# Second network of a fused attention kernel: when the second batch is transposed, in which order the first pair's products run, and which engine makes sums and low parts

## The chip, the cores and the metric

The kernel runs on one core of a Trainium2 chip. The metric is the device time of one execution in microseconds (us). The core has a matrix engine (TensorE, PE in the profile; PEld is its loading of weights), three engines for elementwise work (VectorE or DVE, ScalarE or ACT, GpSimd or POOL) and a queue for transfers (SyncE or SP). Each engine works off its own instructions in order and waits by semaphores for the others. Matrix products go into PSUM, from which VectorE and ScalarE read; everything else lies in SBUF.

## The reference

Attention over 512 local and 32 global rows in each of 4 batches, then two feed-forward networks. The change touches the second one alone:

```python
def _moe2_ref(x, w_in, conv_w, w_out):      # x: (4, 544, 512), d_ff = 1024
    h = np.maximum(x @ w_in, 0.0)
    hp = np.concatenate([zeros, h, zeros], axis=1)
    conv_out = sum(conv_w[k][None, None, :] * hp[:, k:k + S, :] for k in range(3))
    gate = 1.0 / (1.0 + np.exp(-conv_out))
    return (h * gate @ w_out).astype(np.float32)
```

All is float32. A product is made from high and low parts in a reduced float32 format (float32r): w_hi x_hi + w_hi x_lo + w_lo x_hi, three matmuls for one.

## The kernel before

Attention and the first network fill the span up to some 543 us. Each finished block of 128 rows of the first network is scaled and added by VectorE (L741) and stored to the scratch tensor `yscr` in memory (`store_y`, L690, SP's queue); the 32 global rows of each batch are stored there too. The last two blocks belong to batch 3.

The second network goes through the batches 0 to 3, and in each through four pairs `p` of hidden blocks of 128 channels (`NPR` = 4, so 16 pairs, called pair 0 to pair 15 here). For a batch, its 544 rows must lie transposed, as channels by rows. `y_load` (L875) brings a block of rows from `yscr` into `yr` (three buffers), `y_part` (L880) transposes it with four TensorE instructions (L886) into PSUM, from which ScalarE copies it to `yT` (L888). A batch has five blocks, 32 rows and four of 128. Batch 0 is transposed and prepared within the first network. For batch b + 1, pair 0 of batch b loads the blocks 0 to 2 and pair 1 the blocks 3 and 4 (`YP`, L1085); in each pair `turn()` takes one block after T1, one after B22 and one after the output block that follows.

The product x @ w_in of a pair is made in a form with seven instead of eight partial products, each of two 272-column halves: sums of the rows' quarters (`y_sums`, L903: T3, T2, T1 and T4, each 128x544) and of the weights' quarters are made first. For batches 1 to 3 GpSimd makes these sums at the head of pair 2. Then in pair 3, as soon as a product of the old batch is done, ScalarE makes the high part of the new batch's factor and VectorE or (T3, T4, B22) GpSimd the low part (`y_split`, L915), in the place of the old.

`hidden` (L1015) is one pair: the products B11, T2, T3, T1, T4, B21, B22, each six matmuls at L999, with additions between them on VectorE (L1029, L1034, L1039, L1044, L1054) and ScalarE (L1024, L1049). T4 goes on in the PSUM bank of T3 after L1034 has read it (u3), B21 in that of B11, B22 in that of T1. The additions are put 60 instructions ahead in priority (`ahead(B_ADD)`). The tile scheduler orders each engine's instructions by readiness and priority; only TensorE's order in the second network is held to the program's (`keep_order`). `issue_after` (through `behind`) puts an instruction behind another in the issue order of one engine without waiting for its end: the products come behind `mark["first"]`, the last matmul of the last hidden block of the first network.

`gate` (L1001) then makes, for each of the pair's two hidden blocks, the three-tap convolution (L1003 ScalarE, L1004 and L1005 VectorE), the sigmoid (L1006 ScalarE, whose function table is loaded before the first), the product with h (L1007 VectorE), the high part `gh` (ScalarE) and the low part `gl` (GpSimd, both by `split`, L115). `output` (L1073) multiplies a hidden block with its rows of w_out: twelve matmuls (L1061 and L1062 take `gh`, L1063 `gl`). In pair i the output of hidden block 2i - 3 stands between T1 and T4, and that of 2i - 2 after B22. At the end stand the output of the last blocks, that of the global rows of all batches together (`orem`), the copies out of PSUM and the stores.

## Time and profile before

| | us |
|---|---|
| median of 3 runs | 749.65 (749.33 to 752.72) |
| profiled execution | 747.93 |
| its span, first to last instruction | 746.1 |
| TensorE busy in the span | 725.2 (97%) |
| VectorE, ScalarE, GpSimd busy | 490.7, 411.1, 261.1 |
| granted TensorE clock, mean | 0.995 |

The profile is of one execution. The chain of waits goes back from the last instruction to what released each one; the timeline lists instructions by start; windows give each engine's busy time and the granted clock in a stretch of the span. Matmuls overlap, so the distance from one to the next counts and not the length of one. "issue" is time in which the engine named waited for nothing that the profile shows as an instruction of another engine.

### The profile page before, as it was taken

The page shows a single profiled execution, that of the slowest core. Times are in us where ns is not written, and L with a number is a line of the kernel's source. Part 1 is how long each engine was busy: PE and PEld are TensorE (multiplying, and loading weights), DVE is VectorE, ACT ScalarE, POOL GpSimd, SP SyncE. Part 2 cuts the span into 40 slices and gives each one's busy share as a digit, 9 for nine tenths or more (in the row PEclk, how much of TensorE's full clock was granted, in tenths as well). Part 3 has the DMA queues.
Part 4 walks back from the last instruction along what each step waited for, and adds up shares of the span by engine and source line. Part 5 has one row for each costly group of instructions (what it writes and reads, how often), then busy time and mean ns, then how long its engine had stood idle before and what let it go on. Part 6 is the DMA issues. An engine that isn't in the chain of part 4 may idle for free.

```text
span 746.1 us, 13077 instructions
## 1 busy us (share of the span) xinstructions
PE 725.2 (97%) x4745; PEld 650.7 (87%) x4745; DVE 490.7 (66%) x1077; ACT 411.1 (55%) x951; POOL 261.1 (35%) x301
## 2 busy tenths in 40 slices
PE   9999999999999999999999999999959999999997
PEld 5778899999899999999999999988948888888985
DVE  4889974655767666665567526726738969869651
ACT  6768743545565655555445423425545675666742
POOL 1013032434444443444334300002327646565331
PEclk9999999999999999999999999999989999999999
DMA  9992241323333433343232103135121030110101
GB/s 370 424 412 83 57 159 33 118 86 100 111 101 104 120 109 95 84 135 90 80 92 85 36 1 127 58 109 192 58 91 29 1 117 1 29 56 1 58 1 70
DMA packets 31120, 76.18 MB, mean 102 GB/s; under 512 B 3776, under 2 KB 10704, under 8 KB 28496
## 3 DMA queue, kind: packets, MB, share of 16 engines
q1 hardware_dynamic: 30528, 74.52, 30.2%
q8 instruction: 37, 0.61, 0.3%
q10 hardware_dynamic: 528, 0.84, 0.3%
q14 instruction: 27, 0.22, 0.1%
HBM read 66.43 MB, written 8.91 MB: 101 GB/s over the span
## 4 chain that ended last, share of the span: by engine, by line
PE 56%; DVE 6%; issue 5%; ACT 3%; POOL 2%; DMA 1%; ACTq 0%; DVEq 0%; POOLq 0%; SPq 0%
PE ph L709 17%; PE yps L733 6%; PE yps L738 6%; PE yps L734 5%; DVE c L1005 2%; PE pv L999 2%; PE po L337 2%; PE po L1063 2%; PE po L1061 2%; PE po L1062 2%; PE pt L316 2%; POOL gl L115 1%; PE pz L999 1%; PE px L999 1%; DVE c L1004 1%
## 5 line engine op out<-in xcount | busy, mean ns | idle before, releaser
L709 PE MATMUL ph<-xe,w 128*128 128x256 f32 (+1 forms) x768 | 119.8, 298 | 0.9 <-ACT w L159 0.9
L115 POOL TENSOR_TENSOR kl<-raw,kh 128x448 fp32r<-128x448 f32 (+2 forms) x59 | 70.6, 1196 | 133.8 <-ACT kh L108 110.7
L709 PEld LDWEIGHTS ph<-xe,w 128*128 128x128 f32 x768 | 108.4, 188 | 6.2 <-ACT w L159 1.2
L733 PE MATMUL yps<-w,hh 128*128 128x512 f32 x272 | 110.5, 406 | 0.9 <-ACT hh L718 0.4
L709 PE MATMUL ph<-xo,w 128*128 128x256 f32 x768 | 108.2, 284 | 0.0
L734 PE MATMUL yps<-w,hh 128*128 128x512 f32 x272 | 107.7, 396 | 0.0
L709 PEld LDWEIGHTS ph<-xo,w 128*128 128x128 f32 x768 | 101.0, 188 | 4.1
L718 ACT ACTIVATE hh<-ph 128x256 fp32r<-128x256 f32 (+1 forms) x128 | 50.1, 393 | 65.4 <-PE ph L709 59.7
L719 DVE SCALAR_TENSOR_TENSOR hl<-ph,hh 128x256 fp32r<-128x256 f32 x112 | 46.6, 417 | 54.1 <-ACT hh L718 53.1
L115 POOL TENSOR_TENSOR gl<-c,gh 128x544 fp32r<-128x544 f32 x32 | 45.4, 1419 | 78.9 <-ACT gh L108 78.9
L738 PE MATMUL yps<-w,hl 128*128 128x512 f32 x224 | 72.5, 398 | 0.0
L303 ACT ACTIVATE sm<-sm,nm 128x192 f32<-128x192 f32 (+1 forms) x128 | 58.6, 460 | 12.3 <-DVE nm L294 12.0
L294 DVE CUSTOM_DVE_ANT_0 sm<-ps,mask 128x192 f32<-128x192 f32 (+1 forms) x128 | 42.5, 368 | 33.6 <-PE ps L291 22.8
L108 ACT ACTIVATE kh<-raw 128x448 fp32r<-128x448 f32 (+2 forms) x59 | 34.3, 581 | 45.7 <-issue 26.8
L733 PEld LDWEIGHTS yps<-w,hh 128*128 128x128 f32 x272 | 51.2, 188 | 8.8 <-ACT hh L718 1.8
L734 PEld LDWEIGHTS yps<-w,hh 128*128 128x128 f32 x272 | 51.3, 188 | 5.6
L1061 PE MATMUL po<-w,gh 128*128 128x512 f32 x128 | 51.1, 399 | 0.0
L1063 PE MATMUL po<-w,gl 128*128 128x512 f32 x128 | 50.6, 395 | 0.5 <-POOL gl L115 0.5
L1062 PE MATMUL po<-w,gh 128*128 128x512 f32 x128 | 50.7, 396 | 0.0
L261 POOL TENSOR_TENSOR qs<-raw,qs 64x256 fp32r<-64x256 f32 x43 | 33.6, 782 | 46.4 <-DVE qs L260 17.6
L738 PEld LDWEIGHTS yps<-w,hl 128*128 128x128 f32 x224 | 41.1, 188 | 8.7
L321 ACT ACTIVATE ptsb<-pt 128x384 f32<-128x384 f32 (+1 forms) x64 | 34.3, 538 | 25.1 <-PE pt L316 24.6
(186 smaller groups left out, 1572.0 us busy)
## 6 DMA issues: line engine op xcount, KB each, us to landing
wraw<-w SPq DMA_DIRECT2D x16, 1024.0 KB, 16.9
raw<-a_m SPq DMA_DIRECT2D x23, 352.0 KB, 3.0
raw<-a_e SPq DMA_DIRECT2D x20, 320.0 KB, 2.9
raw<-g_qk SPq DMA_DIRECT2D x16, 304.0 KB, 2.8
rawg<-g_v SPq DMA_DIRECT2D x16, 280.0 KB, 2.9
wraw<-w_in SPq DMA_DIRECT2D x8, 512.0 KB, 3.6
yr<-yscr SPq DMA_DIRECT2D x16, 256.0 KB, 2.7
wraw<-w_out SPq DMA_DIRECT2D x4, 1024.0 KB, 7.3
```

What stands on the lines that cost most here:

```text
L115: e_lo.tensor_tensor(lo, src, f32(hi), op=ALU.subtract)
L294: DVE.tensor_tensor_reduce(out=s, in0=ps[j][:, :w], in1=mask[:, self.m0:self.m0 + w], scale=-0.125, scalar=BIG, op0=ALU.add, op1=ALU.min, ...
L303: ACT.activation(s, s, AF.Exp, bias=self.nm[:, j:j + 1], scale=-1.0, accum_out=xt.sums[:, h:h + 1])
L709: e = PE.matmul(ph[:, :n], w[:, d * P:(d + 1) * P], x[:, d], start=m == 0, stop=m == 3 * NDC - 1)
L718: ACT.activation(hh, ph[:, :n], AF.Relu)
L719: DVE.scalar_tensor_tensor(hl, ph[:, :n], 0.0, f32(hh), op0=ALU.max, op1=ALU.subtract)
L733: PE.matmul(yps[i], hh[:, tk], wh[:, DM:], start=edge(k, -1), stop=False)
L734: PE.matmul(yps[i], hh[:, tk], wl[:, DM:], start=False, stop=False)
L738: PE.matmul(yps[i], hl[:, tk], wh[:, DM:], start=False, stop=edge(k, 1))
L1061: PE.matmul(o, gh, wh, start=first, stop=False)
L1062: PE.matmul(o, gh, wl, start=False, stop=False)
L1063: PE.matmul(o, gl, wh, start=False, stop=last)
```

## The change

`B_ADD` is 300 and not 60. `mark["last"]` is the last matmul of the first network's second layer; the products from T3 on come behind it in TensorE's order, B11 and T2 behind `mark["first"]` as before. For batch 1 the loads and transposes begin in pair 1 with two blocks (0 and 1) and end in pair 2 with three; for batches 2 and 3 they stay in the first two pairs of the batch before. The sums are made by VectorE: for batch 1 all four at B11 of pair 3, for the others one at each product from B11 on in the third pair of the batch before. In pair 0 the product B21 comes ahead of T4. In pair 15 VectorE makes the low parts `gl` of both gates.

```diff
--- before.py
+++ after.py
@@ -53,7 +53,7 @@
 HOLD = 2
 HB2 = 2
 PREP = 220
-B_ADD = 60
+B_ADD = 300
 
 XB = 4
 PTB = 2
@@ -735,7 +735,7 @@
 
             for i, key in enumerate(chunks[ci]):
                 tk = slice(i * P, (i + 1) * P)
-                PE.matmul(yps[i], hl[:, tk], wh[:, DM:], start=False, stop=edge(k, 1))
+                mark["last"] = PE.matmul(yps[i], hl[:, tk], wh[:, DM:], start=False, stop=edge(k, 1)).ins
                 if edge(k, 1):
                     x = xtiles[key].x
                     DVE.scalar_tensor_tensor(x, yps[i], xtiles[key].rstd, x, op0=ALU.mult, op1=ALU.add)
@@ -900,17 +900,17 @@
             parts.append(slots2[i // 3][:, i % 3])
         yc[n] = parts
 
-    def y_sums(yT, t, e):
+    def y_sums(yT, t):
 
         ya, yb = [y[:, d] for y, _ in yT for d in (slice(0, 2), slice(2, 4))] if len(yT) == 1 else [y for y, _ in yT]
         u0, u1 = slice(0, HB), slice(HB, S)
         b11, b12, b21, b22 = ya[:, :, u0], ya[:, :, u1], yb[:, :, u0], yb[:, :, u1]
         t3, t2, t4 = t
         ysrc.update({"B11": b11, "T2": t2, "T3": t3, "T1": b12, "T4": t4, "B21": b21, "B22": b22})
-        return [lambda: e.tensor_tensor(t3, b22, b12, op=ALU.subtract),
-                lambda: e.tensor_tensor(t2, t3, b11, op=ALU.add),
-                lambda: e.tensor_tensor(b12, b12, b11, op=ALU.subtract),
-                lambda: e.tensor_tensor(t4, b21, t2, op=ALU.subtract)]
+        return [lambda: DVE.tensor_tensor(t3, b22, b12, op=ALU.subtract),
+                lambda: DVE.tensor_tensor(t2, t3, b11, op=ALU.add),
+                lambda: DVE.tensor_tensor(b12, b12, b11, op=ALU.subtract),
+                lambda: DVE.tensor_tensor(t4, b21, t2, op=ALU.subtract)]
 
     def y_split(n):
         split(*yc[n], ysrc[n], ACT, POOL if Y_NAMES.index(n) in (2, 4, 6) else DVE)
@@ -926,7 +926,7 @@
     def y0_sums(k):
         if k == 0:
             t = wpool.tile([P, 3, 2, HB], F32, tag="w4", name="yt")
-            ysrc["ops"] = y_sums(yT0, [t[:, i] for i in range(3)], DVE)
+            ysrc["ops"] = y_sums(yT0, [t[:, i] for i in range(3)])
         ysrc["ops"][k]()
 
     def y0_split(n):
@@ -988,17 +988,17 @@
     gts, ops = {}, {}
     U0, U1 = slice(1, 1 + HB), slice(1 + HB, 1 + S)
 
-    def product(ps, w, k, n, start):
+    def product(ps, w, k, n, start, key="last"):
 
         yh, yl = yc[n]
         for d in range(2):
             c = slice(k * EIGHTH + d * P, k * EIGHTH + (d + 1) * P)
             wh, wl = w[:, 0, c], w[:, 1, c]
             for m, (wx_, y) in enumerate(((wh, yh), (wh, yl), (wl, yh))):
-                with behind("first"):
+                with behind(key):
                     PE.matmul(ps, wx_, y[:, d], start=start and d + m == 0, stop=d + m == 3, skip_group_check=True)
 
-    def gate(b, f, h):
+    def gate(b, f, h, e=POOL):
         c = gpool.tile([P, S], F32, tag="c", name="c")
         ACT.activation(c, h[:, 0:S], AF.Copy, scale=cw[:, 3 * f:3 * f + 1])
         DVE.scalar_tensor_tensor(c, h[:, 1:S + 1], cw[:, 3 * f + 1:3 * f + 2], c, op0=ALU.mult, op1=ALU.add)
@@ -1007,7 +1007,7 @@
         DVE.tensor_tensor(c, h[:, 1:S + 1], c, op=ALU.mult)
         gh = gpool.tile([P, S], F32R, tag="gh", name="gh", bufs=4)
         gl = gpool.tile([P, S], F32R, tag="gl", name="gl", bufs=4)
-        split(gh, gl, c, ACT, POOL)
+        split(gh, gl, c, ACT, e)
         POOL.tensor_copy(grem_h[:, f, b * SG:(b + 1) * SG], f32(gh[:, :SG]))
         POOL.tensor_copy(grem_l[:, f, b * SG:(b + 1) * SG], f32(gl[:, :SG]))
         gts[b, f] = gh, gl
@@ -1018,13 +1018,14 @@
         n = b * NPR + p
         he, ho = hs[2 * n % 4], hs[(2 * n + 1) % 4]
         p1s, u2, u3 = (us[:, n % 2 * 3 + i] for i in range(3))
+        e = DVE if n == B * NPR - 1 else POOL
         px = ps_x.tile([P, HB], F32, tag="px", name="px")
-        product(px, a, 0, "B11", True)
+        product(px, a, 0, "B11", True, "first")
         with ahead(B_ADD):
             ACT.activation(p1s, px, AF.Copy)
         at("B11")
         py = ps_x.tile([P, HB], F32, tag="py", name="py")
-        product(py, x, 1, "T2", True)
+        product(py, x, 1, "T2", True, "first")
         with ahead(B_ADD):
             DVE.tensor_tensor(u2, py, p1s, op=ALU.add)
         at("T2")
@@ -1039,22 +1040,29 @@
             DVE.tensor_tensor(he[:, U1], pz, u3, op=ALU.add)
         at("T1")
         at(0)
-        product(pv, a, 3, "T4", False)
-        with ahead(B_ADD):
-            DVE.tensor_tensor(he[:, U0], pv, u2, op=ALU.add)
-        ACT.activation(he[:, 1:1 + S], he[:, 1:1 + S], AF.Relu)
-        at("T4")
-        product(px, a, 1, "B21", False)
-        with ahead(B_ADD):
-            ACT.activation(ho[:, U0], px, AF.Relu)
-        at("B21")
-        gate(b, 2 * p, he)
+
+        def t4():
+            product(pv, a, 3, "T4", False)
+            with ahead(B_ADD):
+                DVE.tensor_tensor(he[:, U0], pv, u2, op=ALU.add)
+            ACT.activation(he[:, 1:1 + S], he[:, 1:1 + S], AF.Relu)
+            at("T4")
+
+        def b21():
+            product(px, a, 1, "B21", False)
+            with ahead(B_ADD):
+                ACT.activation(ho[:, U0], px, AF.Relu)
+            at("B21")
+
+        for part in (t4, b21) if n else (b21, t4):
+            part()
+        gate(b, 2 * p, he, e)
         product(pz, x, 2, "B22", False)
         with ahead(B_ADD):
             DVE.tensor_tensor(ho[:, U1], pz, u2, op=ALU.add)
         ACT.activation(ho[:, U1], ho[:, U1], AF.Relu)
         at("B22")
-        gate(b, 2 * p + 1, ho)
+        gate(b, 2 * p + 1, ho, e)
 
     def mm_o(o, gh, gl, f, first, last):
         wh, wl = (w[:, f % 2 * DM:(f % 2 + 1) * DM] for w in wt["o", f // 2])
@@ -1082,20 +1090,24 @@
                 (ACT if e is DVE else SP).dma_start(out[b, SG + t * P:SG + (t + 1) * P, :], emit(ops[b][t], e))
 
     steps = [(b, f) for b in range(B) for f in range(NF2)]
-    YP = [(0, 1, 2), (3, 4)]
     second = len(traced())
+    yT, sums, parts = None, [], []
     for i in range(B * NPR):
         b, p = divmod(i, NPR)
         more = b + 1 < B
-        if more and p == 0:
-            yT = [(gpool.tile([P, NDC, S], F32, tag="yT", name="yT", bufs=1), slice(0, NDC))]
-        parts = list(YP[p]) if more and p < 2 else []
-        for k in parts:
-            y_load(b + 1, k, gpool, "yr", 3)
-        if more and p == 2:
-            t = [gpool.tile([P, 2, HB], F32, tag=f"yt{k}", name="yt", bufs=1) for k in range(3)]
-            for op in y_sums(yT, t, POOL):
-                op()
+        if more:
+            k = p - (b == 0)
+            if k == 0:
+                yT = [(gpool.tile([P, NDC, S], F32, tag="yT", name="yT", bufs=1), slice(0, NDC))]
+                todo = list(range(NT + 1))
+            if 0 <= k < 2:
+                n = 2 if b == 0 and k == 0 else 3
+                parts, todo = todo[:n], todo[n:]
+                for x in parts:
+                    y_load(b + 1, x, gpool, "yr", 3)
+            if k == 2:
+                t = [gpool.tile([P, 2, HB], F32, tag=f"yt{k}", name="yt", bufs=1) for k in range(3)]
+                sums = y_sums(yT, t)
 
         def turn():
             if parts:
@@ -1106,7 +1118,13 @@
                 if 2 * i >= 3:
                     output(*steps[2 * i - 3])
                 turn()
-            elif more and p == 3:
+                return
+            if sums:
+                sums.pop(0)()
+                if more and p == 3 and n == "B11":
+                    while sums:
+                        sums.pop(0)()
+            if more and p == 3:
                 y_split(n)
 
         hidden(b, p, at)
@@ -1114,6 +1132,7 @@
         if 2 * i >= 2:
             output(*steps[2 * i - 2])
         turn()
+        assert not parts
     output(*steps[-3])
     o = ps_v.tile([P, DM], F32, tag="pv", name="orem")
     output(*steps[-2])
```

## Rows read from the trace of the kernel before

**Rows 1.** The page, part 1: busy time, share, instructions.

```profile
PE 725.2 (97%) x4745; PEld 650.7 (87%) x4745; DVE 490.7 (66%) x1077; ACT 411.1 (55%) x951; POOL 261.1 (35%) x301
```

**Rows 2.** Chain of waits, 545 us: start, length, engine, tile, line.

```profile
543.79 1.40 DVE x L741 x2
545.22 2.02 DMA yscr<-x
547.24 2.40 issue
```

**Rows 3.** Windows, mostly by pair: stretch, length, engines' busy time, clock, DMA.

```profile
543.66:549.64 5.98, 0.00 (x2) 0.03 (x1) 2.32 (x5) 0.84 (x1) 2.60 (x2) 0.82 0.40 125
549.64:567.50 17.86, 15.03 (x92) 13.98 (x93) 9.68 (x15) 11.94 (x21) 5.64 (x8) 0.87 0.27 83
567.50:579.20 11.70, 11.12 (x68) 9.67 (x67) 10.35 (x13) 5.98 (x11) 9.27 (x9) 1.00 0.00 1
579.20:590.04 10.84, 10.84 (x67) 9.75 (x66) 9.69 (x13) 8.32 (x16) 7.24 (x8) 1.00 0.01 2
...
661.06:672.80 11.74, 11.16 (x68) 9.71 (x67) 10.39 (x13) 6.02 (x11) 9.27 (x9) 1.00 0.00 1
...
716.20:727.04 10.84, 10.84 (x67) 9.75 (x66) 6.43 (x12) 5.49 (x11) 3.45 (x6) 1.00 0.00 0
```

**Rows 4.** Chain of waits: one product, one transposed block of 128 rows.

```profile
579.36 0.75 PE px L999 x6
...
598.82 0.44 PE pty L886 x4
```

**Rows 5.** Windows of 2 us, the clock: pause's end, and 559.

```profile
548.00:550.00 2.00, 0.36 (x4) 0.39 (x4) 0.00 (x0) 0.00 (x0) 0.00 (x0) 0.50 0.67 176
...
558.00:560.00 2.00, 0.77 (x6) 0.78 (x7) 1.28 (x2) 1.97 (x5) 0.00 (x0) 1.00 0.00 0
```

**Rows 6.** Timeline, first gate: start, length, engine, line, operation, [idle before].

```profile
551.94 0.44 DVE L1044 TENSOR_TENSOR hs<-pv,us 128x272 f32<-128x272 f32 x1 [5.86 <-PE pv L999]
...
555.00 0.77 DVE L1005 SCALAR_TENSOR_TENSOR c<-hs,cw,c 128x544 f32<-128x544 f32 x1
...
556.74 1.28 ACT L1006 ACT_TABLE_LOAD   x1
...
558.03 0.66 ACT L1006 ACTIVATE c<-c 128x544 f32<-128x544 f32 x1
...
559.23 1.01 PE L999 MATMUL py<-yc,wx 128*128 128x272 f32 x6 [2.15 <-ACT yT L888]
...
560.22 1.37 POOL L115 TENSOR_TENSOR gl<-c,gh 128x544 fp32r<-128x544 f32 x1 [13.01 <-ACT gh L108]
```

**Rows 7.** Timeline, pair 15: a low part, the output taking it.

```profile
729.57 1.35 POOL L115 TENSOR_TENSOR gl<-c,gh 128x544 fp32r<-128x544 f32 x1 [7.40 <-ACT gh L108]
...
730.98 0.50 PE L1063 MATMUL po<-w,gl 128*128 128x512 f32 x1 [0.51 <-POOL gl L115]
```

**Rows 8.** Timeline, VectorE at the pause: the add making u3.

```profile
545.11 0.43 DVE L1034 TENSOR_TENSOR us<-pv,us 128x272 f32<-128x272 f32 x1
```

**Rows 9.** Groups by line, 540 to 746: count, busy us, mean ns.

```profile
L1029 DVE TENSOR_TENSOR us<-py,us 128x272 f32<-128x272 f32 x16 | 7.0, 435 | 2.4 <-PE py L999 2.4
...
L115 DVE TENSOR_TENSOR yc<-yt,yc 128x544 fp32r<-128x544 f32 x3 | 2.2, 717 | 0.0
```

**Rows 10.** Timeline, a steady pair's gate: add, low part, output.

```profile
712.10 0.44 DVE L1044 TENSOR_TENSOR hs<-pv,us 128x272 f32<-128x272 f32 x1 [3.02 <-PE pv L999]
...
718.72 1.53 POOL L115 TENSOR_TENSOR gl<-c,gh 128x544 fp32r<-128x544 f32 x1 [7.39 <-ACT gh L108]
...
724.71 0.40 PE L1063 MATMUL po<-w,gl 128*128 128x512 f32 x1
```

**Rows 11.** Timeline, pair 2: GpSimd's first sum, VectorE beside it, T4's wait.

```profile
565.60 1.48 POOL L910 TENSOR_TENSOR yt<-yT 128x544 f32<-128x544 f32 x1 [0.49 <-ACT yT L888]
...
565.89 1.78 DVE L1005 SCALAR_TENSOR_TENSOR c<-hs,cw,c 128x544 f32<-128x544 f32 x1
...
571.20 1.89 DVE L1005 SCALAR_TENSOR_TENSOR c<-hs,cw,c 128x544 f32<-128x544 f32 x1
...
574.04 1.02 PE L999 MATMUL pv<-yc,wae 128*128 128x272 f32 x6 [0.58 <-DVE us L1034]
```

## The prediction

> **What bounds the kernel now.** I read the page's busy times first: TensorE shows as busy for 97% of the span [rows 1], so a gain can only come from its pauses, and those have to be looked for stage by stage. The chain of waits shows one outright: its only long stretch without work on an engine is at 543.8 to 549.6 us, in the first of the 16 hidden-layer pairs of the second network [rows 2]. The chain there is a VectorE finish of the first network's last rows, their store to memory, then the load of the next batch's first rows, which the transposes at L886 need. Third, I cut the rest of the span into stretches from one pair's first product to the next [rows 3]. A pair without transposes takes 10.84 us (the last row). One product (six matmuls) starts 0.75 us after the one before, and one transposed row block takes 0.44 [rows 4]; a pair is seven products and two output blocks, so an output block is (10.84 - 5.25)/2 = 2.80. The stretches that exceed their own work are where time is lost:
> - From the end of pair 0's fourth product (543.66) to the first product of pair 2 (567.50) 23.84 us pass. The work in it is 3 + 7 products, five transposes and one output block: 7.50 + 2.20 + 2.80 = 12.50. Lost: 11.34. Of it 5.98 is the pause, in which TensorE does nothing; after it the granted clock is 0.50 (1.2 GHz of 2.4), where it had been 1.00 [rows 5]. Another 2.15 is a wait of L999 for the copy out of the transposes at 559.2, with the clock at 1.00 all round it [rows 5, 6]; the other 3.2 is mostly the half clock.
> - Pairs 2, 6 and 10 take 11.70, 11.70 and 11.74, so each loses about 0.88 (pair 6 is like pair 10) [rows 3]. In these GpSimd makes the next batch's sums.
> - At the end TensorE waits 0.51 us for GpSimd's last low parts at L1063 [rows 7].
>
> Together that is 11.34 + 2.6 + 0.5 = 14.5 us: no edit to these places can bring more.
>
> **The change, part by part.**
>
> *Transposes a pair later (batch 1 only), with pair 0's B21 ahead of T4.* Pair 0 loses its two transposes, pair 1 keeps two, pair 2 has three, and the sums fall into pair 3. Nothing of TensorE's work is removed; the pause loses its cause, because pair 0's last three products need nothing from memory. What comes next in line? T4 needs the sum u3 of L1034, which VectorE makes only at 545.11 to 545.54, since it stands behind the finish of L741 [rows 2, 8]. B21 fills 543.66 to 544.41. If the add is not sooner, T4 waits 1.1 us; B_ADD = 300 puts it ahead of older work in priority, so it may come right after its product, at no wait. Without that wait, pair 0 ends at 545.9, pair 1's four first products at 548.9, and the first transpose then waits for the load, which lands at 549.64 as before: 0.7 us. (The five loads move with their transposes. SP's queue has the two stores in front of them, as before, and behind them only the loads of batch 2, due four pairs later; ScalarE's five copies out of the transposes move into pairs where it is busy 5.98 of 11.70 [rows 3].) With that wait, the load has landed when TensorE comes. So one of the two, 0.7; bounds 0 and 1.2.
>
> Then pair 1 goes on: transpose 0.44, three products 2.25, transpose 0.44, so the output block of channel block 0 is reached at 552.8. It needs `gh` and `gl` of the first gate. That chain took 9.6 us in the profile, from L1044 at 551.94 to the end of `gl` at 561.59 [rows 6], and held nobody up there, as TensorE reached that output later still. Now it starts at about 545.3 and ends at 555.0, while L1063 is due at 553.3: a new wait of 1.7 to 1.8 us. That is the cover which the old pause gave and which is gone. Bounds: nothing, if the table load inside it comes sooner (L1005 ended at 555.77, the sigmoid began only at 558.03); 4.7, if pair 1's three adds (0.44 each, [rows 9]) and 1.6 us of ScalarE work get between. I take 1.8, as the chain's own row is the nearest. Waits of about 2 us did not lower the clock [rows 5, 6], so no half clock.
>
> ScalarE's sigmoid table is loaded in that chain, and the row gives 1.28 us, with the next activation 0.01 us after its end [rows 6]. The Trainium skill, "ScalarE: Activation LUTs", section "What ACT_TABLE_LOAD costs", adds 1.38 us of drain, about 2.66 in all. By it the wait would be 1.4 longer and my sum 1.4 us later, between my forecast and rival B; the trace shows no such drain, so it gets no chance of its own.
>
> Sum to pair 2: 11.18 of work (10 products, two transposes, one output block) + 0.7 + 1.8 = 13.68. Pair 2 with three transposes: 10.84 + 1.32 = 12.16. Pair 3 gets four sums on VectorE, ahead of seven splits. A sum with both inputs in SBUF takes 0.72 there (the same tile shape at L115) [rows 9], 2.9 us in all, to 9.69 of 10.84 already busy [rows 3]: 12.6, or 1.75 over. An add for TensorE has priority over it, and a gate has about 4.5 us of slack: in a steady pair `gl` ends at 720.25 and L1063 takes it at 724.71 [rows 10]. So 0 to 2.0, and I take 0.5, nearer the slack: 11.34. Sum 37.18, against 23.84 + 11.70 + 10.84 = 46.38 before. Gain 9.2.
>
> *VectorE instead of GpSimd for the sums.* While GpSimd's four sums run (the first 1.48), four gate operations of VectorE take 1.78 (the first) to 1.89 (the last) instead of 0.77 [rows 6, 11]: 4 x 1.07 = 4.3 us of blocking per batch, after which the adds are late and T4 waits 0.58 [rows 11]. VectorE pays 2.9 of its own and is rid of 4.3. For batches 2 and 3 the sums now go out one per product through pair 2, whose VectorE was busy 10.35 us [rows 3]: 10.35 - 4.3 + 2.9 = 9.0 of 10.84. Gain 0.88 in each of pairs 6 and 10, less 0.2 each for sums that stand before an add: 1.3. Bounds 0 and 1.76.
>
> The Trainium skill speaks against this edit: "SBUF — State Buffer", "Who interferes with whom", says a VectorE instruction with two SBUF inputs and a GpSimd one that reads SBUF block each other for the whole instruction, whichever starts first, and its summary advises to schedule whichever is off the critical path. By that the sums on VectorE can be blocked in turn by a `gl` of GpSimd. That the blocking exists the stretched rows agree with [rows 11]; what it makes of the time is rival C.
>
> *Last pair's low parts on VectorE.* `gl` takes 1.35 on GpSimd [rows 7] and about 0.72 on VectorE, which has nothing else left then. L1063 waits 0.51 now: gain 0.5, bounds 0 and 0.6.
>
> *Products behind the last matmul of the first network.* T3 and later now come after the last L738, not between the L733s. It is the same work in another order, with B11 and T2 still there to cover the wait for `hh`: nothing. Were the cover too thin, under 1 us, as TensorE shows no pause there now. B_ADD in the other pairs: nothing, as a steady pair is already full; the bad side is rival D.
>
> Total 9.2 + 1.3 + 0.5 = 11.0. The profiled execution took 747.93 (span 746.1); the median of the runs shown is 749.65, 1.7 above. I take the gain off the median: 738.6.
>
> **Rivals.**
> - B: *the gate becomes the pause.* For it: the chain's 9.6 us has no cover left, and VectorE and ScalarE have pair 1's work at the same time. If TensorE waits 4.7 us, that is near the 5.98 that halved the clock. Cost 2.9 more, and about 2.7 for a half clock after it (three products and a transposed block at twice their time): gain 5.4, 744.2. Against: two-microsecond waits left the clock alone. The edit not doing what it says ends here too: if pair 0's rest waits for something else until about 549, hidden so far by the load, the gain is near 6.
> - C: *the shared reads move instead of going.* Each VectorE sum is blocked by a `gl` (1.35); 4 x (0.72 + 1.35) = 8.3 exceeds the 4.3 it is rid of. Pairs 6 and 10 gain nothing (-1.3), and pair 3 loses 2.0, not 0.5. Gain 8.2: 741.4.
> - D, *slower: adds parked at the head of VectorE's queue.* With priority 300 an add is queued before gate work though its product isn't done. VectorE stands 3.02 us before L1044 in a steady pair already [rows 10]. If gates come so late that TensorE waits more than 11.0/15 = 0.73 us in each of the 15 following pairs, the kernel is slower; at 1.0 per pair it takes 738.6 + 15 = 753.6. Against: the slack of 4.5 us has to be used up first.
>
> **How the numbers follow.** Forecast 738.6: 0.60. B 0.20, C 0.15, D 0.05. The range needs the forecast with its bounds, C and the better half of B: below, all but 0.4 of the 14.5 us gained, 735.5; above, 744.0. About 0.5% (3.7 us) is what a measurement can tell from no change. Faster by more: forecast, C and nearly all of B, 0.91; within 0.5%: the rest of B and a mild D, 0.06; slower 0.03.
>
> **What would show it.** In the profile after: no pause of 6 us near 545 and no granted clock of 0.50 behind it; L886's first transposes in pair 1, near 549.6; L1063 or L1061 of the first output block waiting under 2.5 us for `gl` or `gh`; pairs 6 and 10 at 10.9 to 11.0 and no VectorE gate operation of 1.8 beside a sum; pair 3 under 11.5; the last L1063 without a wait. A pause over 4 us at the first output block, or steady pairs above 11.2, would prove me wrong.

## The result and the profile after

The changed kernel takes 741.18 us (median of 4 runs, 741.01 to 741.56); the kernel before, on the same chip, 749.49 (4 runs, 748.03 to 752.72). The ratio is 0.9884, 95% interval 0.9852 to 0.9916: faster by 1.2%, 8.3 us. The two profiled executions lie 6.4 apart (747.93 and 741.56), since the one of before is among its quicker runs: before scatters upwards (747.67 to 752.37 in 13 runs on another chip), and its runs above 749.2 there all show a lower mean clock (0.988 to 0.993, against 0.995). The account below is made between the two spans, 746.15 and 739.77.

The line numbers behind L735 move a little: the add for u3 is L1035 (L1034 before), the one for the upper half of `he` L1040 (L1039), T4's add L1047 (L1044), the output's three matmuls L1069 to L1071 (L1061 to L1063), the sums L910 to L913 as before.

Windows of after, as in [rows 3] (stretch, length, busy time of TensorE, its weight load, VectorE, ScalarE and GpSimd, clock, DMA): from the end of pair 0's fourth product to pair 2, pair 2, pair 3, pair 6.

```profile
543.33:558.77 15.44, 12.12 (x82) 10.56 (x81) 11.03 (x20) 10.78 (x19) 7.22 (x8) 1.00 0.34 106
558.77:570.88 12.11, 12.11 (x79) 10.91 (x78) 7.81 (x14) 7.29 (x13) 3.81 (x7) 1.00 0.11 28
570.88:586.09 15.21, 12.94 (x69) 11.26 (x68) 13.82 (x19) 9.73 (x18) 10.12 (x9) 0.89 0.08 19
610.31:621.15 10.84, 10.84 (x67) 9.75 (x66) 8.51 (x15) 5.79 (x11) 3.95 (x6) 1.00 0.00 1
```

The first row takes the place of 5.98 + 17.86 in [rows 3]; the clock is 1.00 all through. Pair 2 is as long as a steady pair and its three transposes. Pair 6 is a steady pair now, as is pair 10. Pair 3 is the surprise: 4.37 longer than before, TensorE idle for 2.27 of it and the clock at 0.89. (The expectations of e2 to e4 have 15.13 for pair 3 and 13.74 for VectorE in it, read between bounds some 0.2 later.)

Timeline of after, TensorE, all waits above 0.2 us between 541 and 585 (start, length, engine, line, operation, [idle before]):

```profile
545.59 1.02 PE L999 MATMUL pv<-yc,wae 128*128 128x272 f32 x6 [1.36 <-DVE us L1035]
551.96 1.02 PE L999 MATMUL pv<-yc,wae 128*128 128x272 f32 x6 [1.24 <-DVE us L1035]
554.16 1.01 PE L999 MATMUL pz<-yc,wx 128*128 128x272 f32 x6 [0.44 <-DVE hs L1040]
556.35 0.50 PE L1071 MATMUL po<-w,gl 128*128 128x512 f32 x1 [0.27 <-POOL gl L115]
580.89 1.54 PE L999 MATMUL pz<-yc,wx 128*128 128x272 f32 x6 [2.27 <-DVE hs L1040]
```

The load is awaited nowhere. Four waits for VectorE and GpSimd, 3.3 us in all, stand where the pause and the half clock were; the fifth is pair 3's. What VectorE did ahead of the first of them (timeline of after):

```profile
543.18 0.69 DVE L817 TENSOR_TENSOR wae<-wab,wae 128x512 fp32r<-128x512 f32 x1 [1.67 <-ACT wae L814]
543.79 1.40 DVE L741 SCALAR_TENSOR_TENSOR x<-yps,rstd,x 128x512 f32<-128x512 f32 x2
545.11 0.43 DVE L1035 TENSOR_TENSOR us<-pv,us 128x272 f32<-128x272 f32 x1
```

The add starts at 545.11, the same moment as before [rows 8]. At the head of the row stands L817, the low part of the last pair's weights, which waits 1.67 for ScalarE's high part while the finish and the add, both ready, queue behind it. ScalarE's part (L814) had itself waited 2.26 for GpSimd.

Timeline of after, VectorE in pair 3, up to the add that B22 waits for:

```profile
573.31 1.03 DVE L911 TENSOR_TENSOR yt<-yt,yT 128x544 f32<-128x544 f32 x1
574.26 0.72 DVE L912 TENSOR_TENSOR yT<-yT 128x544 f32<-128x544 f32 x1
574.91 0.72 DVE L115 TENSOR_TENSOR yc<-yT,yc 128x544 fp32r<-128x544 f32 x1
575.56 0.43 DVE L1035 TENSOR_TENSOR us<-pv,us 128x272 f32<-128x272 f32 x1
575.91 1.53 DVE L1007 TENSOR_TENSOR c<-hs,c 128x544 f32<-128x544 f32 x1
577.36 0.71 DVE L913 TENSOR_TENSOR yt<-yT,yt 128x544 f32<-128x544 f32 x1
578.00 0.71 DVE L115 TENSOR_TENSOR yc<-yt,yc 128x544 fp32r<-128x544 f32 x1
578.63 1.85 DVE L115 TENSOR_TENSOR yc<-yT,yc 128x544 fp32r<-128x544 f32 x1
580.41 0.43 DVE L1040 TENSOR_TENSOR hs<-pz,us 128x272 f32<-128x272 f32 x1
```

The reader is to see the gap between L1035 and L1040: a gate operation, a sum and two low parts stand in it, and the last one (T1's) takes 1.85 where 0.72 would do, as GpSimd makes a `gl` from 578.21 to 579.91. Then the clock (windows of after, the clock is the third figure from the end):

```profile
580.00:582.00 2.00, 1.10 (x5) 1.11 (x6) 2.00 (x4) 0.66 (x1) 2.00 (x3) 0.79 0.03 8
582.00:584.00 2.00, 2.00 (x7) 1.63 (x7) 1.08 (x3) 1.53 (x3) 1.30 (x2) 0.50 0.01 4
584.00:586.00 2.00, 2.00 (x9) 1.64 (x8) 1.96 (x3) 0.85 (x3) 0.56 (x1) 0.86 0.00 0
```

The account, predicted and measured: the early stretch +10.16 and +8.40; pair 2 -0.46 and -0.41; pair 3 -0.50 and -4.37; pairs 6 and 10 +1.3 and +1.71; the end (last pair's first product to the end of the span, 29.95 before and 29.22 after) +0.5 and +0.73. Together 11.0 and 6.1; another 0.33 lies ahead of the early stretch, 0.19 of it ahead of pair 0, where nothing was changed.

### The profile page after: what moved, and what is told of

It is laid out like the page before. It is cut to its first block, busy times and chain, and to the rows that moved or that the text cites. A ratio compares the mean times of both kernels' runs of the same rounds, so it can differ in the third digit from the quotient of the medians.

```text
span 739.8 us, 13078 instructions
## 1 busy us (share of the span) xinstructions
PE 724.3 (98%) x4745; PEld 650.4 (88%) x4745; DVE 485.1 (66%) x1091; ACT 411.3 (56%) x951; POOL 239.1 (32%) x287
## 4 chain that ended last, share of the span: by engine, by line
PE 68%; DVE 2%; ACT 1%; DMA 1%; POOL 0%; issue 0%; ACTq 0%; SPq 0%
PE ph L709 17%; PE yps L733 6%; PE yps L738 6%; PE yps L734 6%; PE po L1071 4%; PE po L1069 4%; PE po L1070 4%; PE pz L999 3%; PE pv L999 3%; PE px L999 3%; PE po L337 2%; PE pt L316 2%; PE py L999 2%; PE pty L886 1%; PE ps L291 1%; PE pog L422 1%
## 5 line engine op out<-in xcount | busy, mean ns | idle before, releaser
L733 PE MATMUL yps<-w,hh 128*128 128x512 f32 x272 | 110.6, 406 | 0.9 <-ACT hh L718 0.4
L115 POOL TENSOR_TENSOR gl<-c,gh 128x544 fp32r<-128x544 f32 x30 | 42.4, 1415 | 95.0 <-ACT gh L108 95.0
L303 ACT ACTIVATE sm<-sm,nm 128x192 f32<-128x192 f32 (+1 forms) x128 | 58.7, 460 | 11.9 <-DVE nm L294 11.7
L733 PEld LDWEIGHTS yps<-w,hh 128*128 128x128 f32 x272 | 51.3, 188 | 8.7 <-ACT hh L718 1.8
L1069 PE MATMUL po<-w,gh 128*128 128x512 f32 x128 | 51.7, 404 | 0.0
L1071 PE MATMUL po<-w,gl 128*128 128x512 f32 x128 | 51.1, 399 | 0.3 <-POOL gl L115 0.3
```

What stands on the lines that cost most here:

```text
L115: e_lo.tensor_tensor(lo, src, f32(hi), op=ALU.subtract)
L303: ACT.activation(s, s, AF.Exp, bias=self.nm[:, j:j + 1], scale=-1.0, accum_out=xt.sums[:, h:h + 1])
L733: PE.matmul(yps[i], hh[:, tk], wh[:, DM:], start=edge(k, -1), stop=False)
L1069: PE.matmul(o, gh, wh, start=first, stop=False)
L1071: PE.matmul(o, gl, wh, start=False, stop=last)
```

## The experiments

Eleven kernels, in three groups, each group on one chip with runs of the kernel before (medians 749.14, 749.58 and 748.64). Ratios are to before on that chip. Pair 0 begins between 539.15 and 540.56 in the profiled executions, though no edit lies ahead of it, so single executions are compared by stretches. The first four take the change apart and follow up pair 3; the next four the early stretch; the last three the small steps and the gate.

**e1: the later transposes alone.** The kernel before with batch 1's transposes a pair later; the order of products, the sums on GpSimd and the low parts as before.

```diff
+            k = p - (b == 0)
...
-            for op in y_sums(yT, t, POOL):
+                sums = y_sums(yT, t, POOL if True else DVE)
```

> The kernel before with one part of the change alone: batch 1's blocks are loaded and transposed a pair later, and its sums (on GpSimd, as before) stand at the head of pair 3. Theory 1: the shift carries most of the gain, since it takes the 6 us pause and the half clock behind it away: 8 to 10 us of the 23.84 us between 543.7 and pair 2 become work or short waits, the pairs 6 and 10 keep 0.9 us each and the end its 0.5; pair 3 now has the sums and the splits, 1 to 2 us more: 741 to 744. Rival: without the other parts the rest of pair 0 waits for something else (T4 behind the late add, gates without cover), and less than half of the gain is left: 746 to 748.

Measured 747.13 (745.42 to 748.47, 10 runs), ratio 0.9966, 0.995 to 0.9982. The rival's number: the move alone brings 2.0. The profile is of the slowest of the ten. The pause is gone, and T4 waits 2.35 in its place; but pair 1 has a half clock (last section), and pair 4 takes 18.02 instead of 12.22. Its rows (timeline of e1, VectorE and TensorE; this kernel's lines are those of after):

```profile
587.69 1.78 DVE L1005 SCALAR_TENSOR_TENSOR c<-hs,cw,c 128x544 f32<-128x544 f32 x1
589.39 1.88 DVE L1004 SCALAR_TENSOR_TENSOR c<-hs,cw,c 128x544 f32<-128x544 f32 x1
...
592.64 0.43 DVE L1030 TENSOR_TENSOR us<-py,us 128x272 f32<-128x272 f32 x1
...
593.13 0.54 PE L886 MATMUL pty<-ident,yr 32*128 32x32 f32 x4 [2.37 <-DVE us L1030]
```

Two stretched gate operations, beside GpSimd's low parts (586.99 to 588.88 and 588.85 to 590.69), stand ahead of the add. With GpSimd's sums in pair 3, GpSimd's own low parts come late, into the gates of the next pair. The clock fell to 0.50 for 6.8 us behind that wait.

**e2: everything but the later transposes.**

```diff
-            k = p - (b == 0)
+            k = p
...
-                n = 2 if b == 0 and k == 0 else 3
+                n = 3
```

> The changed kernel with the shift alone undone: batch 1 is transposed in pairs 0 and 1 again. Theory 1: the pause of 6 us and the clock of 0.50 are back, but pair 3 is rid of the sums (its 15.13 us become 10.9): 744 to 747. Rival (what was gained came from sums, priority and low parts): 741 to 743, pause or not.

Measured 744.96 (744.76 to 745.84), ratio 0.9946, 0.9926 to 0.9966: as expected, the other edits bring 4.2. The pause is there, 6.16 long. The row to look at is pair 2 (windows of e2), in which batch 1's sums stand one behind each product, as they do for the later batches:

```profile
567.68:578.52 10.84, 10.84 (x67) 9.75 (x66) 8.49 (x15) 5.76 (x11) 3.97 (x6) 1.00 0.00 0
```

Before, pair 2 took 11.70 with VectorE busy for 10.35 [rows 3]; here 10.84 and 8.49. So VectorE can make the sums at no cost, where they have a pair of their own. In the changed kernel batch 1's have not: they fall into the pair of the seven splits.

**e3: batch 1's sums on GpSimd, the rest as changed.**

```diff
-                sums = y_sums(yT, t)
+                sums = y_sums(yT, t, POOL if b == 0 else DVE)
+                while sums and b == 0:
+                    sums.pop(0)()
```

> The changed kernel with batch 1's four sums on GpSimd at the head of pair 3; batches 2 and 3 stay on VectorE. Theory 2: pair 3 takes 15.13 us because VectorE has the four sums ahead of the splits and the add L1040 comes behind them; without them L1040 waits under 1 us, the clock stays at 1.00, and pair 3 takes 11 to 13: 738 to 740. Rival: whoever makes the sums there, the splits come too late and the shared reads are full; GpSimd's sums are slower (1.5 to 1.9 us each), TensorE waits at the next batch's B11 or T3 instead: 741 to 744.

Measured 743.38 (742.76 to 744.69), ratio 0.9925, 0.9903 to 0.9946: the rival's number, worse than the change by 2.2 on the medians (of two chips). Pair 3 falls to 11.13, but pair 4 takes 16.91, with the same wait as in e1 (2.37 for L1030) and a half clock of 3.4 us. What the sums cost in pair 3 they cost in pair 4, and more, on GpSimd: 28.04 for the two pairs, against 27.43. So the loss doesn't go with the engine that makes the sums; it moves to the next pair.

**e4: one low part moved.** The changed kernel with T1's low part behind the add at L1040, in pair 3 of batch 0 alone. On VectorE these two instructions change places, and up to there nothing else; behind them the add of B22 comes ahead of B21's low part as well, and a few later operations change places.

```diff
-            DVE.tensor_tensor(he[:, U1], pz, u3, op=ALU.add)
+            mark["he"] = DVE.tensor_tensor(he[:, U1], pz, u3, op=ALU.add).ins
...
-                y_split(n)
+                with behind("he") if b == 0 and n in ("T1",) else nullcontext():
+                    y_split(n)
```

> The changed kernel with one edge more: in pair 3 of batch 0 VectorE's low part of T1 is put behind the add L1040 in VectorE's order. It swaps these two instructions and leaves the rest of VectorE's order up to there as it is. Theory 2a: the place of one add makes the whole loss of pair 3: L1040 runs 1.85 us sooner, B22 waits 0.4 instead of 2.27, the clock stays at 1.00, pair 3 takes 11.3 to 11.8 instead of 15.13: 737.3 to 738.2. Rival 2b: VectorE is simply overfull there (13.74 us busy in pair 3) and the wait turns up at the next add or gate: 740.3 to 741.5.

Measured 739.09 (738.91 to 739.39), ratio 0.9866, 0.9846 to 0.9885. Timeline of e4 in pair 3:

```profile
579.12 0.71 DVE L115 TENSOR_TENSOR yc<-yt,yc 128x544 fp32r<-128x544 f32 x1
579.75 0.43 DVE L1040 TENSOR_TENSOR hs<-pz,us 128x272 f32<-128x272 f32 x1
580.11 1.52 DVE L115 TENSOR_TENSOR yc<-yT,yc 128x544 fp32r<-128x544 f32 x1
580.24 1.01 PE L999 MATMUL pz<-yc,wx 128*128 128x272 f32 x6 [0.49 <-DVE hs L1040]
```

And its window of pair 3:

```profile
572.00:583.88 11.88, 11.39 (x69) 9.93 (x68) 11.39 (x17) 9.13 (x17) 9.02 (x9) 1.00 0.09 24
```

The wait falls from 2.27 to 0.49, the clock stays at 1.00, and the pair takes 11.88. The low part is still stretched (1.52), but nobody waits for it there. This shows the cause of most of pair 3's loss, 3.33 of 4.37: not the amount of work on VectorE but one stretched instruction ahead of an add, and the half clock that came behind the wait. (The two profiled spans differ by only 2.2, as pair 0 begins 1.2 later in e4's.)

**e5: B_ADD back at 60.**

```diff
-B_ADD = 300
+B_ADD = 60
```

> The changed kernel with B_ADD back at 60. Its instructions stand in the same order on all five engines as in the changed kernel, so theory 1 (300 moves nothing that 60 doesn't) expects the time of the changed kernel, 741.2 within 0.5, with the same waits: T4 of pair 0 1.3 to 1.4 us for the u3 add, pair 3 at 15.2. Theory 2 (300 put the adds ahead) expects T4 to wait 1 us longer and 742 to 743.

Measured 741.61 (741.25 to 743.00), ratio 0.9888, 0.9865 to 0.991, T4's wait 1.39, pair 3 15.20. The instructions stand in the same order on every engine as in the changed kernel; this edit of the change does nothing, and the run is one more of the changed kernel, to which e6, e9 and e11 are compared.

**e6: B21 behind T4 again in pair 0.**

```diff
-        for part in (t4, b21) if n else (b21, t4):
+        for part in (t4, b21):
```

> The changed kernel with B21 behind T4 again in pair 0. T4 then comes 0.75 us sooner to the same u3 add, which stands behind the first network's finish on VectorE, so it waits 1.36 + 0.75 = 2.1 us. Theory 1 (the product between them is worth its own length): 0.75 later, 741.9. Theory 2 (the first output block waits anyway for the gate, which starts with T4's add, and that add comes no later): what is lost at T4 is saved there, 741.2 within 0.3. Theory 3 (a pause of 2.1 us lowers the clock, as 2.27 did in pair 3): 743 to 745, with a granted clock of 0.50 near 548.

Measured 742.06 (741.48 to 742.89), ratio 0.9894, 0.9869 to 0.9919: 0.45 from e5, within the spread of both. From pair 0's first product to pair 2's both take 19.61: T4 waits 2.09 and pair 0 takes 8.90 (8.03 in e5), but pair 1 takes 10.71 (11.58), as its waits at B22 and at the output are gone. The median, 742.06, is nearer the first theory's number; the trace shows what the second says: the swap only moves the wait. The clock stayed at 1.00 behind the 2.09.

**e9: the weight low part behind the u3 add.** L817 of the last pair, on VectorE, behind L1035 of pair 0 instead of ahead of the finish.

```diff
+                if p == NPR - 1 and e is DVE and c.start:
+                    held1.append(ins)
...
+        for ins in held1 if n == 0 else []:
+            tc.add_manual_dep(ins, mark["u3"].name, mybir.DependencyInfo(
+                mybir.DependencyClass.NoSync, mybir.DependencyReason.DATA), reason="order")
```

> The changed kernel with VectorE's last low part of the first network's weights (L817, last pair) behind the u3 add of pair 0 instead of ahead of it, so that the two finishes of L741 and the u3 add come sooner by its duration. Theory 1 (T4 has its u3 sooner and nothing else is late): T4 waits 0.7 less, 740.5. Theory 2 (the load of the next batch's rows, at about 549.6, is then awaited by the first transpose): T4's wait goes and one of about as much comes at L886, 741.2 within 0.3.

Measured 738.79 (738.26 to 742.31), ratio 0.9863, 0.9834 to 0.9893: more than either theory gave it. Two things make it more. L817 had held the finish up for its wait for ScalarE too, not only for its own 0.69: pairs 0 and 1 take 17.81, against 19.61 in e5. The other is luck: in the profiled execution the clock didn't fall in pair 3 (13.66, against 15.20), which the edit doesn't touch, and two of the five runs, 742.14 and 742.31, are no faster than e5. Timeline of e9 (L742 is the finish, L819 the low part, L1077 and L1079 the output's first and third matmul):

```profile
541.74 1.41 DVE L742 SCALAR_TENSOR_TENSOR x<-yps,rstd,x 128x512 f32<-128x512 f32 x2 [0.24 <-PE yps L739]
543.42 1.11 DVE L819 TENSOR_TENSOR wae<-wab,wae 128x512 fp32r<-128x512 f32 x1
553.10 0.50 PE L1077 MATMUL po<-w,gh 128*128 128x512 f32 x1 [0.88 <-ACT gh L108]
554.52 0.50 PE L1079 MATMUL po<-w,gl 128*128 128x512 f32 x1 [0.69 <-POOL gl L115]
```

And its window from the end of pair 0's fourth product to pair 2:

```profile
543.27:556.96 13.69, 12.12 (x83) 10.60 (x81) 9.66 (x17) 10.25 (x18) 5.83 (x6) 1.00 0.38 120
```

The finish starts 2.05 earlier than in after (0.13 of it as pair 0 begins that much earlier), T4 and the transposes wait for nothing, and the whole wait lies where the prediction had put it, at the first output block: 1.57 (predicted 1.8). The stretch takes 13.69 (predicted 13.68), but that is partly a coincidence: 12.12 of work and 1.57 of waits, where the prediction had 11.18 and 2.5. VectorE's order behind the moved instruction changed too: pair 1's add at L1040 (L1048 here) now comes ahead of a convolution and of the first product with h.

**e11: e9, and three operations of pair 3 moved.** e9 and e4 together, with the fourth sum and T2's low part behind L1040 as well.

```diff
+        for ins in held2 if n == NPR - 1 else []:
+            tc.add_manual_dep(ins, mark["he"].name, mybir.DependencyInfo(
+                mybir.DependencyClass.NoSync, mybir.DependencyReason.DATA), reason="order")
...
+                    if b == 0 and n == "T2":
+                        held2.extend(x for x in traced()[at0:] if x.engine == mybir.EngineType.DVE)
```

> The changed kernel with the weight low part behind the u3 add in pair 0, and in pair 3 the fourth sum and the low parts of T2 and T1 behind the upper half's add at L1040. Theory 1 (what is left of pair 3's excess over 10.84, 11.88 with T1's low part alone moved, is sums and splits ahead of that add): pair 3 at 10.9 to 11.2, no clock below 1.00 behind it, 736.5 to 738. Theory 2 (the low parts moved behind come too late for pair 4's products, or for the gates): pair 3 at 11.8 or more, or pair 4 over 12.5, 738.5 to 740.

Measured 736.18 (735.50 to 736.91), ratio 0.9812, 0.9787 to 0.9837. Pair 3 (window of e11):

```profile
570.14:581.28 11.14, 11.14 (x70) 9.90 (x68) 10.73 (x16) 7.89 (x15) 8.28 (x7) 1.00 0.09 25
```

TensorE is busy in all of it, as the first theory expected, though the time is a little better than its 736.5. Pair 4 takes 12.22, as in after, so nothing came too late. Against e4, with the clock at 1.00 in both, pairs 0 and 1 take 17.88 instead of 19.41: 1.5 for L817's place, free of the clock.

**e7: GpSimd makes the last pair's low parts again.**

```diff
-        e = DVE if n == B * NPR - 1 else POOL
+        e = POOL
```

> The changed kernel with GpSimd making the low parts of the last pair's two gates again. Theory 1 (the last output block waits for the second of them): the wait for gl at the last output block is 0.5 instead of 0.3 and the tail from the last pair's first product to the end 29.8 to 29.9 instead of 29.25; 741.7 to 741.9. Theory 2 (VectorE's low part is not much sooner, since the first of them took 1.57 there and not 0.72): no difference that the profile shows, 741.2 to 741.5.

Measured 742.57 (742.28 to 743.71), ratio 0.992, 0.9904 to 0.9936. TensorE in the last pair, timeline of e7:

```profile
725.36 0.50 PE L1071 MATMUL po<-w,gl 128*128 128x512 f32 x1 [0.51 <-POOL gl L115]
```

The wait of [rows 7] is back, and the tail takes 29.91 instead of 29.22. The edit is worth 0.69. (The median is 0.7 above the range expected, and e8's, on the same chip, 0.6 above that of its first theory; no wait in either trace answers to that.)

**e8: all products behind the first matmul of L733 again.**

```diff
-    def product(ps, w, k, n, start, key="last"):
+    def product(ps, w, k, n, start, key="first"):
```

> The changed kernel with all products held behind the first matmul of L733 again, so that the five matmuls of pair 0's third product stand among the first network's last matmuls and not behind them. Theory 1 (the same work in another order, nothing waits): 741.2 to 741.6, no new wait on TensorE. Theory 2 (the first network's last matmuls then come about 0.6 later, and with them the finish that the u3 add stands behind): T4 of pair 0 waits 0.6 longer, 741.8 to 742.2.

Measured 742.24 (740.59 to 742.90), ratio 0.9911, 0.9893 to 0.9928. T4 waits 1.43 (1.36 in after, 1.39 in e5), not the 0.6 more of the second theory, whose time the median nearly has; every pair is as long as in after within 0.1, and pair 0 begins 1.17 later. No difference that the trace shows.

**e12: e11, with the sigmoid's table loaded early.** One sigmoid of a single column, behind pair 0's first copy; its output is overwritten later.

```diff
             ACT.activation(p1s, px, AF.Copy)
+        if n == 0:
+            with ahead(B_ADD):
+                ACT.activation(us[:, 5, 0:1], p1s[:, 0:1], AF.Sigmoid)
```

> The kernel with the weight low part behind the u3 add and the three VectorE operations of pair 3 moved (736.18 measured), and one sigmoid of a single column behind pair 0's first copy, so that ScalarE loads the sigmoid's table (1.28) there, where it is idle, and not inside the first gate, on which the first output block then waits 0.90 and 0.70. Theory 1 (the table load is on that chain): the two waits fall from 1.6 to 0.3 to 0.6 together, 734.9 to 735.3. Theory 2 (the chain stands on VectorE's and ScalarE's other work and takes the gap up again, or the load at its new place holds up the weights' copies and with them products): 736.0 to 737.0.

Measured 735.41 (735.16 to 736.27), ratio 0.982, 0.9804 to 0.9837. Timeline of e12, ScalarE, then the one wait that is left in the early stretch (L1086 is the third matmul of the output):

```profile
541.18 0.39 ACT L1031 ACTIVATE us<-px 128x272 f32<-128x272 f32 x1
541.59 1.28 ACT L1034 ACT_TABLE_LOAD   x1
542.89 0.20 ACT L1034 ACTIVATE us<-us 128x1 f32<-128x1 f32 x1
...
554.87 0.50 PE L1086 MATMUL po<-w,gl 128*128 128x512 f32 x1 [0.70 <-POOL gl L115]
```

Pair 1 takes 10.13 instead of 11.17: of the 1.28 that was moved, 1.04 came back, as the wait for `gh` is gone; the one for `gl` stays at 0.70, more than expected. The median is 0.8 below e11's, taken on another chip. This version beats both kernels. By the prediction's bound, 747.93 - 14.5 = 733.4, some 2 us would be left; the trace shows 0.70 of waits and 0.30 in pair 3 (11.14, against 10.84).

## Why the prediction was right and wrong

Predicted were 738.6 us, between 735.5 and 744.0, and faster by more than 0.5% with a chance of 0.91. Measured are 741.18: the direction and the range hold, the time is 2.6 above the forecast. Step by step:

- **What bounds the kernel** was right: all gains came from the places listed, e11 and e12 took 13.4 and 13.2 of the 14.5 on the medians (11.2 and 11.9 between the profiled spans), and the steady pairs stayed at 10.84 to 10.88.
- **"The pause loses its cause"** was right: no pause at 545, clock 1.00, the first transposes at 550.28 without a wait. e1 shows that the later transposes alone take the pause away (with a half clock of 3.4 us in pair 1 there), e2 that nothing else does.
- **"B_ADD = 300 puts it ahead of older work in priority"** is the first step that failed. The value moves nothing (e5), the add came at 545.11 as before, and T4 waited 1.36 (bounds 0 and 1.2). The prediction had named the finish at L741 as what the add stands behind; the one to name was the low part L817 at the head of the queue, waiting for ScalarE (e9). The row for it was in the trace of before, and was not read.
- **"A new wait of 1.7 to 1.8"** at the first output block was right in its mechanism and nearly in size, but not in its place: in after the waits at T4 (1.36 and 1.24) and B22 (0.44) came first and left 0.27 for `gl`. With L817 out of the way, the same wait stood at the output, 1.57 (e9). The 1.24 and 0.44 are a term that was left out of the sum: pair 1's adds stand behind the first gates' convolutions and products on VectorE. So the waits came to 3.3, not 2.5. The work was sized too small as well: 12.12, not 11.18 (in e9's timeline ten products 7.99 and not 7.50, two transposes 0.96 and not 0.88, the output block 3.17 without its waits and not 2.80), since prices of an unbroken row were used where waits and transposes break it. Together the early stretch took 15.44, not 13.68.
- **The gate's chain** took 9.65, from T4's add at 546.64 to the end of `gl` at 556.29, and 9.6 was taken [rows 6]. The table load took 1.28 and the next activation began 0.02 behind it (0.01 before). The Trainium skill, "ScalarE: Activation LUTs", section "What ACT_TABLE_LOAD costs", has 1.38 of drain on top; no row shows it, and moving the load away gave back 1.04 (e12).
- **Pair 3, "0 to 2.0, and I take 0.5"** is the step that was most wrong: 4.37. Its reason, "an add for TensorE has priority over it", doesn't hold: with a priority of 60 and of 300 the splits stand ahead of the add at L1040 (e5), and the slack of 4.5 belongs to the gates, not to the adds. VectorE was busy for 13.82 there, and 12.6 was estimated; but what was not asked is what stands between an add's input and the add. 1.8 of the 4.37 is the wait beyond e4's 0.49, about 1.5 the half clock (15.2 in after and e5, against 13.66 in e9 with the same wait and no fall of the clock), 1.0 what e4 leaves and e11 mostly removes.
- **"Waits of about 2 us did not lower the clock"** is the third step that failed. It rested on one row of 2.15 [rows 6]. See the last section.
- **The sums on VectorE** gained the whole excess of pairs 6 and 10, 1.71 of 1.76; the 0.2 taken off for sums ahead of an add were not paid, and VectorE's busy time fell to 8.51 (9.0 estimated). The Trainium skill's rule ("SBUF — State Buffer", section "Who interferes with whom") that a VectorE instruction with two SBUF inputs contends with a GpSimd one that reads SBUF is borne out by the rows of pair 3, where VectorE's 0.72 becomes 1.85 beside a `gl`. The advice in that page's section "Summary: rules for kernel authors", to schedule whichever is off the critical path, is what e4 follows when it moves the blocked one behind the add.
- **The end** gained 0.73 (0.5 predicted, a little over its bound of 0.6), of which e7 shows 0.69. **Products behind the last matmul: nothing** was right (e8). The swap, which the prediction counted on to fill 0.75 of T4's wait, moves a wait and gains nothing measurable (e6).

Of the rivals, B (the gate as a pause of 4.7) didn't come: that output waits 0.27. C came near with its time, 741.4, but for another reason: pairs 6 and 10 gained in full, and pair 3's loss doesn't come from all sums being blocked, since it goes when one split is moved (e4) and stays, a pair later, when GpSimd makes the sums (e3). D could not come, as the priority moved no instruction.

One more point on sizes: the prediction took a gain worked out on the profiled execution off the median. Between the profiled executions the gain was 6.4, between the medians 8.3. That before's median lay further above its profiled run than after's did hid 1.9 of the error: luck, not insight.

## What to carry to other kernels

When a step is moved, list for each engine what then stands between an add that TensorE waits for and the instruction that makes it ready, with the wait of the first one in that queue: an in-order engine makes all of them late, and a priority that changes no order changes nothing. Move the longest or the blockable one (two inputs in SBUF while GpSimd reads too) behind the add. And cost the move by the pair that receives the work, not by the mean: the same four sums were free in a pair of their own (e2), while the pair that had them along with the splits grew by 4.4 us, 3.3 of which the place of one low part decided (e4).

## What the runs showed of the hardware

A pause of TensorE a little above 2 us was followed by the half clock in some profiles and not in others, at the same place and with the same length. The wait for the add at L1040 (L1048 in e9) in pair 3 was followed by a granted clock of 0.50 in the profiled executions of after (2.27), e5 (2.27), e7 (2.24) and e8 (2.26), and by 1.00 throughout in those of e6 (2.26) and e9 (2.24). Windows of e9 (the wait, and what follows it), to set beside those of after above:

```profile
577.00:579.00 2.00, 0.00 (x0) 0.00 (x0) 2.00 (x3) 0.82 (x2) 2.00 (x3) 1.00 0.00 0
579.00:581.00 2.00, 1.94 (x11) 1.77 (x12) 1.97 (x4) 1.54 (x3) 1.82 (x3) 1.00 0.04 8
581.00:583.00 2.00, 2.00 (x12) 1.64 (x11) 1.51 (x2) 1.50 (x3) 1.22 (x1) 1.00 0.02 4
```

e9's five runs took 738.26, 738.69 and 738.79 with a mean clock of 0.999, and 742.14 and 742.31 with 0.995; e4 and e11, without that pause, kept within 0.5 and 1.4 us. So one kernel gets different mean clocks in its runs; the 3.5 between the two groups is more than the 1.5 of the one fall, and as the slower two were not profiled, where they lost it isn't shown. The Trainium skill, "TensorE: Matmul & The Clock Gate", Part 1, says of the clock's rise at a kernel's start that its place varies between runs of the same kernel; here a fall behind the same pause came in some profiles and not in others. What decides it in one run was not tried. Pauses of 2.09 (e6) and 2.15 (before) were followed by 1.00, those of 2.37 (e1, e3) by 0.50, in the one profile that there is of each.

Nor does the length of one pause decide it alone. In e1 TensorE waited 2.35 for T4 in pair 0, and the clock stayed at 1.00; it fell in pair 1, behind T4's wait of 1.31 there (window of e1):

```profile
556.00:558.00 2.00, 2.00 (x11) 2.00 (x11) 0.21 (x1) 1.49 (x3) 2.00 (x6) 0.50 0.00 0
```

In e6 the waits at the same two places, 2.09 and 1.31, were followed by 1.00.
